# Weight parts of a fused attention and MLP kernel: one slot and one store for a high and low part, casts on ScalarE, later loads and sums

## The chip, the cores and the metric

The kernel runs on one core of one Trainium2 chip. The engines of the core are named as in the profile: PE (TensorE matmul), PEld (its weight loads), DVE (VectorE), ACT (ScalarE), POOL (GpSimd) and SP (SyncE, which issues all DMAs here, one after another). Each engine works through its own instructions strictly in the order in which the program lists them. The metric is the device time in microseconds of one execution; the median of three runs of the kernel before is 1123.24 us (1121.22 to 1124.15).

## The reference

Causal attention with a decay over 8 batches, 8 heads, 576 positions and 64 dimensions, followed by a two-layer MLP over the 4608 tokens:

```python
scores = scale * np.matmul(q, k.transpose(0, 1, 3, 2))
cum = np.cumsum(np.log(np.clip(f, 0.0001, 1.0)), axis=-1)
scores = np.where(causal, -1000000000.0, scores + cum[:, :, :, None] - cum[:, :, None, :])
attn = softmax(scores)                                  # max, exp, sum + 1e-9
x = np.matmul(attn, v) reshaped to (4608, 512)
h = x @ w_in                                            # (4608, 2048)
g = h * erf(np.maximum(h, 0.0) + np.log1p(np.exp(-np.abs(h))))
out = g @ w_out                                         # (4608, 512), float32
```

The weights w_in and w_out are given as float64 and read as pairs of 32-bit words.

## The kernel before, in words

**Attention.** The 64 heads go in 32 pairs, each pair in two steps `t` (even: query blocks 4 and 1, odd: 3, 2 and 0), so there are 64 steps and a tail of 5. It is a pipeline: in step t PE makes the scores of t (`scores`, line 607), DVE reduces them with the decay mask (`reduce`, 630), ACT takes the exponentials of t-1 (`exps`, 644), POOL normalizes t-2 (`normalize`, 651), PE transposes t-3 into one of three PSUM banks (`transposes`, 661), ACT and DVE copy these out (`evacuate`, 672), and PE multiplies t-4 with the values (`values`, 683). The last copy of `evacuate` on ACT must be done before PE's next use of that bank. POOL also makes the mask of step t+1 (`mask`, 592) from the cumulative decays c, which for all pairs but the first are read back from `cum_d`, the sums of all heads that the start of the program writes to memory.

**Early weight work.** One after another, small pieces of work on the weights are put behind the steps: `todo` (lines 516 and 792) has 60 of them, one popped in each step and two in each tenth step. Ten pieces of weights (eight of w_in, two of w_out for half 0) are loaded (`load`), then `magnitude` (ACT), `normal`, `low_bits` and `join` (DVE) turn the 64-bit words into float32, and `parts` (412) splits the result into a high part in float32r and a low part, the rest: the high by a cast, the low by a subtraction on POOL that reads the high part. For w_in four sums of quarters (`sums`) are split too, since the first product is computed by seven smaller products. The buffers of this work are slots xs1, xs2 (raw words), xs3, xs4 (top words) and xs6 (sums); the same slots hold later x's parts 1, 2, 3, 4 and 6. x's first group is read and split in `x_work`, from step 24 in even steps, and `start_x` (545), in steps 59 to 63: its j-th call casts part 1, 4, 6, 2 or 3 on ACT and takes the rest on POOL.

**The MLP.** It runs in units n of `step` (277), four for each of 12 visits v (six groups of tokens, twice, for the two halves of the hidden width; k is n modulo 4). A unit has seven products i = 0 to 6 (`product`), each of six matmuls, with two PSUM banks in turn. Their results are taken out by `consume`: a copy `sa` on ACT at i = 0 (line 194), an addition `sb` on DVE at i = 1, h copied on ACT at i = 2 (199), `sc` and three h on DVE at i = 3 to 6 (205). PE cannot start a product in a bank before the one that was there has been taken out. For the unit before, ACT takes softplus (209) and erf (212), each with its table load, DVE multiplies (215), ACT casts the high part gh (224) and POOL makes the low part gl (225). For the unit before that, PE makes the second product into y (242), six matmuls after each of i = 0, 1, 2, 3, 4 and 6.

What else is done stands in the order written here. `next_x` (128) reads and splits the x of the next visit: two sums by `x_sum` (lines 107 and 109) of the four blocks t0 to t3 that `load_x` has loaded, then casts on ACT and rests on DVE in the last unit of the visit. `late_work` (489) plans the weights of half 1 and the rest of half 0: piece m has a unit n, three places (a, b, c) for `normal`, `low_bits` and `join`, and a unit and place for its parts. In four rounds of four units each, piece pairs of w_in give seven parts (three quarters and four sums), whose casts (420) and subtractions (421) follow each other behind the products i = 3 to 6; they are stored to `wi_d` and read back by `reload` when half 1 begins. Their buffers lhi and llo share four rotating slots, `ws`; a slot is free when the store that reads it is done.

## Time and profile before

| | |
|---|---|
| median of 3 runs | 1123.24 us |
| the profiled execution | 1124.44 us |
| its span, first to last instruction | 1122.7 us |
| busy, share of the span | PE 97%, PEld 84%, DVE 70%, ACT 70%, POOL 47% |
| mean granted clock of TensorE | 0.992 |
| attention | to about 317 us, mixed with the first units to 353 us |
| full units without weight work (700 to 1000 us) | PE busy 300 of 300 us |

Times in the timelines are microseconds from the start of the span. A timeline row gives start, length, engine, line, instruction, the tiles, and in brackets how long the engine sat idle before it and what ended that. A row of waits gives the engine and line that waited, what it waited for, then total us, times and the longest. A row of the groups by form ends with total us and the mean in ns. The rows of the chip's DMAs end with KB each and the median us from issue to landing. A window row gives start and end, length, then the busy us of each engine with the count of instructions, the granted clock of TensorE, and the DMA share and GB/s.

### The profile page before, as it was taken

The page shows a single profiled execution, that of the slowest core. Times are in us where ns is not written, and L with a number is a line of the kernel's source. Part 1 is how long each engine was busy: PE and PEld are TensorE (multiplying, and loading weights), DVE is VectorE, ACT ScalarE, POOL GpSimd, SP SyncE. Part 2 cuts the span into 40 slices and gives each one's busy share as a digit, 9 for nine tenths or more (in the row PEclk, how much of TensorE's full clock was granted, in tenths as well). Part 3 has the DMA queues.
Part 4 walks back from the last instruction along what each step waited for, and adds up shares of the span by engine and source line. Part 5 has one row for each costly group of instructions (what it writes and reads, how often), then busy time and mean ns, then how long its engine had stood idle before and what let it go on. Part 6 is the DMA issues. An engine that isn't in the chain of part 4 may idle for free.

```text
span 1122.7 us, 21302 instructions
## 1 busy us (share of the span) xinstructions
PE 1084.4 (97%) x7384; PEld 945.6 (84%) x7384; DVE 781.1 (70%) x1776; ACT 782.1 (70%) x1718; POOL 533.2 (47%) x733
## 2 busy tenths in 40 slices
PE   8999999999998899998999989999999999999997
PEld 7888888888888788887878879889888988899886
DVE  5898999999855775785757765655656565656543
ACT  4888887878876676767667586666666576756662
POOL 4787979888853343343342533333223332233322
PEclk9999999999998999999999999999999999999999
DMA  7777886677433134152432417442221313040122
GB/s 252 237 244 234 274 271 245 223 246 221 136 111 104 39 130 141 41 176 96 164 118 82 154 48 262 175 176 81 85 85 57 113 57 114 15 138 18 31 82 75
DMA packets 74906, 155.82 MB, mean 139 GB/s; under 512 B 7472, under 2 KB 27184, under 8 KB 73776
## 3 DMA queue, kind: packets, MB, share of 16 engines
q1 hardware_dynamic: 74800, 154.47, 41.2%
q8 instruction: 59, 0.97, 0.3%
q14 instruction: 47, 0.39, 0.1%
HBM read 114.44 MB, written 39.99 MB: 138 GB/s over the span
## 4 chain that ended last, share of the span: by engine, by line
PE 67%; issue 17%; POOL 8%; DMA 3%; DVE 3%; ACT 1%; SPq 0%; POOLq 0%; DVEq 0%; ACTq 0%
PE y L242 22%; PE m L181 20%; PE s L616 8%; PE o L697 8%; PE t L670 7%; POOL gl L225 5%; POOL llo L421 2%; DMA wi_d<-llo 1%; DVE pr L636 1%; DMA xt_d<-xo 1%; PE s L620 1%; POOL wo L421 1%; PE idle L735 0%; DMA lraw<-in_w_out_dram 0%; ACT e L212 0%
## 5 line engine op out<-in xcount | busy, mean ns | idle before, releaser
L225 POOL TENSOR_TENSOR gl<-e,gh 128x384 fp32r<-128x384 f32 x192 | 224.4, 1197 | 489.8 <-ACT gh L224 476.2
L181 PE MATMUL m<-x,wi 128*128 128x384 f32 x2016 | 402.5, 338 | 19.0 <-ACT sa L194 9.2
L181 PEld LDWEIGHTS m<-x,wi 128*128 128x128 f32 x2016 | 358.2, 189 | 52.3 <-DVE h L205 15.0
L242 PE MATMUL y<-wo,gh 128*128 128x512 f32 x1152 | 359.2, 393 | 1.9 <-POOL wo L421 1.2
L242 PEld LDWEIGHTS y<-wo,gh 128*128 128x128 f32 x1152 | 212.7, 188 | 30.5 <-POOL wo L421 1.6
L242 PE MATMUL y<-wo,gl 128*128 128x512 f32 x576 | 228.9, 397 | 0.0
L658 POOL TENSOR_SCALAR pr<-pr,st 128x576 f32<-128x576 f32 (+4 forms) x320 | 165.1, 540 | 46.4 <-DVE st L654 22.3
L648 ACT ACTIVATE pr<-pr,st 128x576 f32<-128x576 f32 (+3 forms) x320 | 176.7, 557 | 5.7 <-DVE st L636 5.7
L215 DVE TENSOR_TENSOR e<-e,h 128x384 f32<-128x384 f32 x192 | 144.4, 793 | 28.2 <-ACT e L212 28.2
L636 DVE CUSTOM_DVE_ANT_0 pr<-s,c 128x576 f32<-128x576 f32 (+3 forms) x320 | 136.4, 486 | 21.8 <-PE s L620 13.8
L209 ACT ACTIVATE e<-h 128x384 f32<-128x384 f32 x192 | 93.4, 520 | 69.6 <-DVE h L205 69.2
L224 ACT CAST gh<-e 128x384 fp32r<-128x384 f32 x192 | 92.0, 512 | 59.6 <-DVE e L215 59.0
L242 PEld LDWEIGHTS y<-wo,gl 128*128 128x128 f32 x576 | 108.2, 188 | 23.0
L616 PE MATMUL s<-k,q 64*128 64x320 f32 (+4 forms) x768 | 110.0, 407 | 3.0 <-DVE st L636 3.0
L679 ACT COPY pt<-t 128x512 f32<-128x512 f32 x128 | 74.1, 579 | 54.5 <-PE t L670 52.4
L197 DVE TENSOR_TENSOR sb<-m,sa 128x384 f32<-128x384 f32 x48 | 26.7, 556 | 122.1 <-PE m L181 76.0
L697 PE MATMUL o<-pt,v 128*64 128x128 f32 (+1 forms) x1920 | 104.1, 261 | 3.7 <-DVE xo L706 2.4
L670 PE MATMUL t<-ident,pr 128*128 128x128 f32 x800 | 104.5, 276 | 3.0 <-ACT pt L679 2.9
L697 PEld LDWEIGHTS o<-pt,v 128*64 128x64 f32 x1920 | 95.2, 139 | 13.8 <-DVE st L636 4.2
L670 PEld LDWEIGHTS t<-ident,pr 128*128 128x128 f32 x800 | 87.4, 140 | 15.2 <-issue 10.7
L616 PEld LDWEIGHTS s<-k,q 64*128 64x128 f32 x768 | 72.6, 186 | 31.4 <-issue 16.7
L122 DVE TENSOR_TENSOR x<-t,x 128x768 fp32r<-128x768 f32 x77 | 80.3, 1054 | 18.9 <-ACT x L117 18.9
(96 smaller groups left out, 1098.3 us busy)
## 6 DMA issues: line engine op xcount, KB each, us to landing
v<-in_vp_dram SPq DMA_DIRECT2D x32, 576.0 KB, 6.9
c<-cum_d SPq DMA_DIRECT2D x62, 288.0 KB, 5.7
t<-xt_d SPq DMA_DIRECT2D x44, 384.0 KB, 5.8
q<-in_q_dram SPq DMA_DIRECT2D x32, 320.0 KB, 3.9
k<-in_k_dram SPq DMA_DIRECT2D x32, 288.0 KB, 4.5
xt_d<-xo SPq DMA_DIRECT2D x32, 288.0 KB, 6.0
part_d<-yo SPq DMA_DIRECT2D x36, 256.0 KB, 4.2
yo<-part_d SPq DMA_DIRECT2D x36, 256.0 KB, 3.1
```

The lines of the kernel that those rows point to most:

```text
L181: nc.tensor.matmul(out=ps, lhsT=w[:, wp, ws], rhs=x[:, xp, kd], start=first and kd == 0 and j == 0, stop=kd == 1 and j == 2 and i in (1, 2 ...
L209: self.nc.scalar.activation(out=e, in_=self.h[n, q], func=AF.Softplus)
L215: self.nc.vector.tensor_mul(self.e[n, q], self.e[n, q], self.h.pop((n, q)))
L224: nc.scalar.copy(out=gh, in_=e)
L225: nc.gpsimd.tensor_tensor(out=gl, in0=e, in1=gh.bitcast(F32), op=ALU.subtract)
L242: yield nc.tensor.matmul(out=y[tb], lhsT=g[:, cs], rhs=w[:, f, wp], start=first, stop=last)
L616: nc.tensor.matmul(out=s[j][:, at:at + k1 - k0], lhsT=q[h, PAD + START[i]:PAD + END[i]], rhs=k[h, k0:k1], start=i > 0, stop=i not in (0, 3))
L636: nc.vector.tensor_tensor_reduce(out=to[:, ::-1] if j else to, in0=score, in1=decay_, scale=-0.125, scalar=BIG, op0=ALU.add, op1=ALU.min, ...
L648: nc.scalar.activation(out=seg, in_=seg, func=AF.Exp, bias=st[:, 0, j, m:m + 1], scale=-1.0, accum_out=st[:, 1, j, m:m + 1])
L658: nc.gpsimd.tensor_scalar(out=seg, in0=seg, scalar1=st[:, 2, j, m:m + 1], scalar2=1.0, op0=ALU.mult, op1=ALU.mult)
L670: nc.tensor.transpose(out=b[:, n * P:(n + 1) * P], in_=probs[t][:, at:at + P], identity=ident)
L697: nc.tensor.matmul(out=o[h, to:to + width], lhsT=v[:, ch, h], rhs=pt[:, at[j]:at[j] + width], start=n == 0, stop=n == len(parts) - 1, skip ...
```

## The change

Five things change; PE's instructions and their order stay as they are.

- **One slot, one store.** For parts of w_in that go to memory, the high and low part are the two halves of one tile `both` (2 KB per partition) in one slot of `ws`, and one DMA of 256 KB stores them, where there were two tiles, two slots and two DMAs of 128 KB.
- **Early casts on ACT.** The high parts of the early weight work are cast by ACT (`nc.scalar.copy`) and not by DVE. At the start, the factor -8 of the decays is applied by ACT too.
- **The start.** q and k of pairs 1 and 2 and the first values are loaded ahead of everything that needs the decays; `load_decay` loads c apart. All three logarithms come first, then all three scans. The early weight work starts at step 6 instead of 3, and its first two loads are issued in steps 3 and 5. So it ends in step 60, where it ended in step 57.
- **x's sums of the second group.** `load_x` loads the blocks of the second 384 tokens (t2, t3) first. For visit 1 the two sums move from behind the products 4 and 5 of unit 2 to behind product 6 of unit 2 and product 0 of unit 3.
- **Weight pieces four and five of the late plan** (counted from 0): `normal`, `low_bits` and `join` of piece 4 move from products 5, 5 and 6 of unit 3 to 0, 0 and 1 of unit 4; those of piece 5 from 2, 2 and 4 of unit 4 to 4, 4 and 5.

```diff
@@ load_x, next_x
-        for j, (token, half) in enumerate([(0, 0), (0, 1), (1, 0), (1, 1)]):
+        for j in (2, 3, 0, 1):
+            token, half = divmod(j, 2)
...
-        if k == 2 and i in ((4, 5) if v == 1 else (0, 1)):
-            self.x_sum(v, i - (4 if v == 1 else 0), dve)
+        for j in range(2):
+            if (k, i) == ([(2, 6), (3, 0)][j] if v == 1 else (2, j)):
+                self.x_sum(v, j, dve)
@@ parts, in_parts
-            width = 512 if cut is None else 2 * P
             if to is not None:
                 hi, lo = to
+            elif cut:
+                both = buf("both", m, [P, 2, 2 * P], F32R)
+                hi, lo = both[:, 0], both[:, 1]
             else:
-                hi, lo = (buf(x, m, [P, width], F32R) for x in ("hi", "lo"))
+                hi, lo = (buf(x, m, [P, 512], F32R) for x in ("hi", "lo"))
...
-            if to is None:
+            if to is None and cut:
+                nc.sync.dma_start(out=dst, in_=both.bitcast(F32))
+            elif to is None:
                 nc.sync.dma_start(out=dst[0], in_=hi.bitcast(F32))
                 nc.sync.dma_start(out=dst[1], in_=lo.bitcast(F32))
@@ late_buf
-        tag, bufs = {"raw": ("raw", 2), "top": ("top", 3), "tt": ("tt", 1), "hi": ("ws", 4), "lo": ("ws", 4)}[kind]
+        tag, bufs = {"raw": ("raw", 2), "top": ("top", 3), "tt": ("tt", 1), "hi": ("ws", 4), "lo": ("ws", 4),
+                     "both": ("ws", 4)}[kind]
@@ early_work, late_work
-            pieces, early_buf, nc.vector.tensor_copy)
+            pieces, early_buf, nc.scalar.copy)
...
-        plan = [(1, first, 2, 1), (1, second, 2, 1), (2, first, 3, 2), (2, second, 3, 3), (3, (5, 5, 6), 4, 2), (4, first, 4, 5)]
+        plan = [(1, first, 2, 1), (1, second, 2, 1), (2, first, 3, 2), (2, second, 3, 3), (4, (0, 0, 1), 4, 2), (4, (4, 4, 5), 4, 5)]
...
-            moe.work[n, "abs"].append(lambda m=m: magnitude(m))
+            moe.work[n - (m == 4), "abs"].append(lambda m=m: magnitude(m))
@@ decay, load, load_decay
-            nc.vector.tensor_scalar(out=out, in0=out, scalar1=-8.0, scalar2=None, op0=ALU.mult)
+            nc.scalar.activation(out=out, in_=out, func=AF.Copy, scale=-8.0)
...
-            c = io.tile([P, 2, S], F32, name=f"c{p}", tag="c")
-            if p:
-                for j in range(2):
-                    n = 2 * p + j
-                    nc.sync.dma_start(out=c[:, j], in_=cum_d[n:n + 1].rearrange("a s -> (a s)").partition_broadcast(P))
-            pairs[p] = [q, k, c]
+            pairs[p] = [q, k, io.tile([P, 2, S], F32, name=f"c{p}", tag="c")]
+
+        def load_decay(p):
+            c = pairs[p][2]
+            for j in range(2):
+                n = 2 * p + j
+                nc.sync.dma_start(out=c[:, j], in_=cum_d[n:n + 1].rearrange("a s -> (a s)").partition_broadcast(P))
@@ the start and the steps
+        for p in (1, 2):
+            load(p)
+        load_values(0)
         idle_products("", 34)
-        log_clipped(fd[0])
-        log_clipped(fr)
+        for x in (fd[0], fr, fd[1]):
+            log_clipped(x)
         decay(pairs[0][2][:, 0], fd[0])
         cum = wk.tile([B * H, S], F32, name="cum", tag="xo")
         decay(cum, fr)
         nc.sync.dma_start(out=cum_d, in_=cum)
-        load(1)
-        load(2)
-        load_weight(0)
-        load_weight(1)
+        for p in (1, 2):
+            load_decay(p)
         mask(0, slice(0, 1))
-        log_clipped(fd[1])
+        decay(pairs[0][2][:, 1], fd[1])
+        mask(0, slice(1, 2))
...
-                if t >= 3 and todo:
+                if t >= 6 and todo:
                     todo.pop(0)()
+            if t in (3, 5):
+                load_weight(t // 2 - 1)
```

Where the order of the instructions moves, three places matter for what follows. Tile names carry the step or unit, then a running number.

The end of attention, on ACT, at the end of step 60 (x0_4 is x's part 4, whose slot is xs4; top9 are the top words of the last weight piece, in the same slot; wo0_0 its high and low part; pr60 the scores of step 60; pt58 the transposed ones of 58). Before:

```order
L679 COPY pt57_5088<-t57_1_5094 128x512
L117 CAST x0_4_5138<-tc_2177 128x768
L648 ACTIVATE pr60_5081,st60_5082<-pr60_5081,st60_5082 128x576
L648 ACTIVATE pr60_5081,st60_5082<-pr60_5081,st60_5082 128x192
L679 COPY pt58_5168<-t58_0_5169 128x512
```

Now:

```order
L688 COPY pt57_5085<-t57_1_5091 128x512
L424 CAST wo0_0_4564<-top9_4891 128x512
L118 CAST x0_4_5138<-tc_2168 128x768
L657 ACTIVATE pr60_5078,st60_5079<-pr60_5078,st60_5079 128x576
L657 ACTIVATE pr60_5078,st60_5079<-pr60_5078,st60_5079 128x192
L688 COPY pt58_5168<-t58_0_5169 128x512
```

The cast of the last weight piece has come in front of x's part 4; that cast now waits on POOL for the subtraction that still reads top9.

The end of unit 2 and the start of unit 3, on DVE (ltop2 and ltop3 are late weight pieces, h2_1 and h2_2 the results of the products 5 and 6, t1_4 and t1_2 the two sums of x). Before:

```order
L107 TENSOR_TENSOR t1_4_5729<-t1_2_5727,t1_3_5728 128x768
L409 SCALAR_TENSOR_TENSOR ltop2_5793<-ltop2_5793,lraw2_5717 128x512
L397 SCALAR_TENSOR_TENSOR ltop3_5795<-ltop3_5795,lraw3_5719 128x512
L205 TENSOR_TENSOR h2_1_5866<-m2_2_5815,sb2_5770 128x384
L109 TENSOR_TENSOR t1_2_5727<-t1_0_5725,t1_2_5727 128x768
L402 TENSOR_SCALAR lraw3_5719<-ltop3_5795 128x512
L404 SCALAR_TENSOR_TENSOR lraw3_5719<-lraw3_5719 128x512
L205 TENSOR_TENSOR h2_2_5877<-m2_3_5840,sb2_5770 128x384
L409 SCALAR_TENSOR_TENSOR ltop3_5795<-ltop3_5795,lraw3_5719 128x512
```

Now:

```order
L411 SCALAR_TENSOR_TENSOR ltop2_5793<-ltop2_5793,lraw2_5717 128x512
L399 SCALAR_TENSOR_TENSOR ltop3_5795<-ltop3_5795,lraw3_5719 128x512
L207 TENSOR_TENSOR h2_1_5865<-m2_2_5815,sb2_5770 128x384
L404 TENSOR_SCALAR lraw3_5719<-ltop3_5795 128x512
L406 SCALAR_TENSOR_TENSOR lraw3_5719<-lraw3_5719 128x512
L207 TENSOR_TENSOR h2_2_5875<-m2_3_5840,sb2_5770 128x384
L108 TENSOR_TENSOR t1_4_5729<-t1_2_5727,t1_3_5728 128x768
L411 SCALAR_TENSOR_TENSOR ltop3_5795<-ltop3_5795,lraw3_5719 128x512
L110 TENSOR_TENSOR t1_2_5727<-t1_0_5725,t1_2_5727 128x768
```

Both sums, which need x from memory, now stand behind both h, which free PE's banks.

The start, on DVE (fd0 and fd1 are the decays of the first two heads, fr those of all heads, c0 and cum their sums). Before:

```order
L563 TENSOR_SCALAR fd0_155<-fd0_155 128x576
L563 TENSOR_SCALAR fr_158<-fr_158 64x576
L568 SCALAR_TENSOR_TENSOR c0_164<-fd0_155 128x576
L569 TENSOR_SCALAR c0_164<-c0_164 128x576
L568 SCALAR_TENSOR_TENSOR cum_207<-fr_158 64x576
L569 TENSOR_SCALAR cum_207<-cum_207 64x576
L563 TENSOR_SCALAR fd1_156<-fd1_156 128x576
```

Now:

```order
L570 TENSOR_SCALAR fd0_155<-fd0_155 128x576
L570 TENSOR_SCALAR fr_158<-fr_158 64x576
L570 TENSOR_SCALAR fd1_156<-fd1_156 128x576
L575 SCALAR_TENSOR_TENSOR c0_164<-fd0_155 128x576
L575 SCALAR_TENSOR_TENSOR cum_221<-fr_158 64x576
L575 SCALAR_TENSOR_TENSOR c0_164<-fd1_156 128x576
```

The clip of fd1 stands ahead of the scans, and the multiplications by -8 are no longer on DVE.

## The prediction

> **What bounds the kernel now.** I read the busy times by stretch first, then the waits of TensorE, then the timelines around its gaps. In attention, from 40 to 280 us:

> ```profile
> 40.00:280.00 240.00, 239.52 (x2784) 199.03 (x2782) 226.28 (x838) 197.37 (x615) 205.58 (x386) 1.00 0.76 246
> ```

> The columns after the length are PE, PEld, DVE, ACT, POOL, then clock and DMA. PE is busy 239.5 of 240 us, so shortening another engine's work buys almost nothing there; DVE is at 94%, ACT at 82%, so DVE is next. What can be won is where PE waits. Its waits over the whole run, longest first, with one of ACT beside them:

> ```profile
> PE m L181 <- ACT sa L194: 9.2, 4, 2.7
> PE m L181 <- DVE h L205: 9.1, 10, 1.5
> ACT pt L679 <- PE t L670: 52.4, 57, 2.5
> ```

> The first row is four gaps of about 2.3 us, the second ten shorter ones. The third says that in attention ACT waits for PE about 0.9 us in nearly every step: ACT has a little slack and not more.

> **The weight rounds (one slot per part).** In each of four rounds, ACT makes seven high parts and POOL seven low ones. Before, each took one of four slots, so two parts were in flight. Round one:

> ```profile
> 432.54 0.71 ACT L420 CAST lhi<-ltop 128x256 fp32r<-128x256 f32 x2
> 435.32 2.07 POOL L421 TENSOR_TENSOR llo<-ltop,lhi 128x256 fp32r<-128x256 f32 x2
> 442.25 0.41 ACT L420 CAST lhi<-ltt 128x256 fp32r<-128x256 f32 x1 [0.79 <-DMA wi_d<-lhi]
> 442.56 0.93 ACT L209 ACTIVATE e<-h 128x384 f32<-128x384 f32 x2
> 443.40 0.46 ACT L194 COPY sa<-m 128x384 f32<-128x384 f32 x1
> 443.91 1.33 PE L181 MATMUL m<-x,wi 128*128 128x384 f32 x6 [2.01 <-ACT sa L194]
> ```

> The seventh cast starts at 442.25, 9.7 us after the first, because each waits for stores; two softplus and the copy sa stand behind it on ACT, and PE, ready at 441.90, waits for sa. Now four casts run at once (done by 434.2), and the fifth needs the store of part one, which needs the low part, which needs POOL. POOL still begins at 435.32; its low parts end at 436.25, 437.4 and, at about 0.9 each, 438.3. The store is one of 256 KB:

> ```profile
> wi_d<-lhi SPq DMA_DIRECT2D x28, 128.0 KB, 1.7
> wo_d<-lhi SPq DMA_DIRECT2D x8, 256.0 KB, 2.3
> part_d<-yo SPq DMA_DIRECT2D x36, 256.0 KB, 4.2
> ```

> The wo_d row has the same size and shape, so 2.3: slots come free at 438.6, 439.7 and 440.6; the seventh cast ends at 441.0, softplus 0.93 later, sa at 442.4. PE then waits 0.5 instead of 2.0. For four rounds: 9.2 - 4 x 0.5 = **7.2 us gained**. Bounds: with 4.2 us (the part_d row) the last slot comes at 442.5 and the gain is 0; with no wait left it is 9.2. The 28 stores fewer cost SP nothing that PE waits for.

> **The first units (x sums, weight pieces five and six).** The chain in units 2, 3 and 4:

> ```profile
> 366.58 1.01 DVE L107 TENSOR_TENSOR t<-t,t 128x768 f32<-128x768 f32 x1 [3.04 <-DMA t<-xt_d]
> 368.72 0.55 DVE L205 TENSOR_TENSOR h<-m,sb 128x384 f32<-128x384 f32 x1
> 369.32 1.33 PE L181 MATMUL m<-x,wi 128*128 128x384 f32 x6 [1.51 <-DVE h L205]
> 387.13 1.75 DVE L397 SCALAR_TENSOR_TENSOR ltop<-ltop,lraw 128x512 f32<-128x512 f32 x1
> 388.38 0.50 PE L242 MATMUL y<-wo,gh 128*128 128x512 f32 x1 [1.17 <-POOL wo L421]
> 389.99 0.55 DVE L205 TENSOR_TENSOR h<-m,sb 128x384 f32<-128x384 f32 x1
> 390.59 1.50 PE L181 MATMUL m<-x,wi 128*128 128x384 f32 x6 [1.48 <-DVE h L205]
> ```

> DVE sits 3.04 us at the sum of x for its load, and h, which frees PE's bank, stands behind it. With the sums behind both h (and tokens' second half loaded first) h is done near 366 and 367.6, PE's 1.51 go, and the sums find their data. Softplus of that h then comes earlier too: erf, gates and POOL's wo parts of unit 3 move about 2 us against 1.5 for PE, so of the 1.17 some 0.5 go. In unit 3 the piece's normal (387.13, 1.75 us) and low bits stood ahead of h at 389.99; they now follow in unit 4, so the 1.48 go. After these gaps PE ran slowly:

> ```profile
> 392.00:394.00 2.00, 2.00 (x6) 1.54 (x5) 1.83 (x4) 1.99 (x4) 0.00 (x0) 0.50 0.44 135
> 394.00:396.00 2.00, 2.00 (x10) 1.84 (x9) 2.00 (x4) 1.43 (x4) 0.00 (x0) 0.76 0.33 127
> 646.00:650.00 4.00, 1.50 (x8) 1.46 (x9) 0.56 (x1) 3.14 (x7) 1.45 (x2) 1.00 0.48 168
> ```

> Granted clock 0.50 and 0.76 for 2 us each: 1.0 + 0.5 = 1.5 us lost, which should not recur without the gaps (the third row, a gap of 2.7 in a round, kept 1.00, so a gap does not always cost it). [...] The trace has 0.50 right behind them, so I keep the row's term. Against it: DVE has no idle time in unit 4, and the moved work puts wo's second piece for unit 5 later there; I take off 0.2. Together 1.5 + 0.5 + 1.5 + 1.5 - 0.2 = **4.8 us gained**; bounds 1.5 (only the first gap) and 5.7.

> **Attention: cast by ACT.** 30 casts leave DVE:

> ```profile
> L420 DVE CAST wi<-tt 128x256 fp32r<-128x256 f32 x16 | 6.9, 470 | 0.0
> ```

> At most 0.47 each, 14 us off an engine that runs beside a full PE. ACT gets about as much; where a cast follows join in the same step, ACT also waits for DVE's join, with the next exponentials behind it. ACT's 0.9 us a step covers most of that. The work starts three steps later, and one step now carries all four sums on DVE. I take +0.3, between -2 and +2. But the last piece now ends in step 60, where it ended in 57, and there it meets x's split. Step 60, and two durations:

> ```profile
> 300.85 0.83 ACT L117 CAST x<-tc 128x768 fp32r<-128x768 f32 x1
> 303.04 0.21 DVE L675 COPY pt<-t 128x64 f32<-128x64 f32 x1
> 303.54 1.82 POOL L122 TENSOR_TENSOR x<-tc,x 128x768 fp32r<-128x768 f32 x1
> 305.05 0.59 ACT L679 COPY pt<-t 128x512 f32<-128x512 f32 x1 [2.15 <-PE t L670]
> 305.33 2.86 POOL L658 TENSOR_SCALAR pr<-pr,st 128x448 f32<-128x448 f32 x6
> 309.60 0.59 ACT L679 COPY pt<-t 128x512 f32<-128x512 f32 x1
> 310.56 1.54 PE L697 MATMUL o<-pt,v 128*64 128x128 f32 x28
> L409 DVE SCALAR_TENSOR_TENSOR top<-top,raw 128x512 int32<-128x512 int32 x10 | 8.9, 890 | 0.0
> L420 ACT CAST lhi<-ltop 128x512 fp32r<-128x512 f32 x8 | 4.9, 616 | 0.0
> L421 POOL TENSOR_TENSOR wo<-top,wo 128x512 fp32r<-128x512 f32 x2 | 2.6, 1280 | 1.4 <-DVE st L653 1.4
> ```

> Slot xs4 holds this piece's top words and then x's part 4. So ACT's cast of x, today at 300.85, waits for POOL's wo, which waits for ACT's cast of wo, which waits for DVE's join, behind the copy at 303.04: 303.25 + 0.89 + 0.62 + 1.28 = 306.1, and the cast of x ends near 307.0. Behind it on ACT stand the exponentials and evacuations of the next step (5.4 us later); on POOL x's rest and then the normalization, 305.33 now, near 308.9 then. It ends at 311.8. The copy at 309.60, which frees the bank for the last transpose ahead of PE's values, ends 8.5 us after the cast of x now, 2.15 of them waiting; with 6.35 of work it ends at 313.4 and values start at 313.5 instead of 310.56: 3.0 us lost. Such a gap costs up to 1.8 us of clock or none (rows above): 0.9. **3.9 us lost**, between 0 (the slack takes it) and 6.

> **The start.** The first clips, and what waits for the decays:

> ```profile
> 2.88 0.43 SPq L722 DMA_DIRECT2D fd<-in_f_dram  x1
> DMA to landing us min/median/max: 4.9/4.9/4.9
> L568 DVE TENSOR_TENSOR_SCAN c<-fd 128x576 f32<-128x576 f32 x2 | 2.7, 1344 | 0.0
> L564 ACT ACTIVATE fd<-fd 128x576 f32<-128x576 f32 x2 | 1.4, 684 | 6.8 <-DVE fd L563 6.8
> 13.52 0.76 DVE L636 CUSTOM_DVE_ANT_0 pr<-s,c 128x576 f32<-128x576 f32 x1 [0.40 <-POOL c L603]
> 18.53 0.88 POOL L603 TENSOR_SCALAR_AFFINE_SELECT c<-c 128x256 f32<-128x256 f32 x2 [3.80 <-DMA c<-cum_d]
> ```

> The third clip now stands ahead of all scans and waits for its load, 2.88 + 4.9 = 7.8; with 0.5 and three scans of 1.34 DVE is at 12.3, ACT scales by 13.0 (0.68), POOL masks, and the second head's reduction starts near 13.6, as today. The store of the sums slips from 9.9 to about 11.7, behind five loads that now go ahead; its readers may land 2 us later than 18.53, where step 2 needs its mask by about 21.5. I take **0.2 lost**, between 2 lost and 0.5 gained.

> **Sum.** 7.2 + 4.8 + 0.3 - 3.9 - 0.2 = 8.2 us. The span of 1122.7 becomes 1114.5; the profiled run was 1124.44, 1.7 more than its span, and 1.2 above the median of 1123.24. On the median: **1115.0 us**.

> **Rivals.**
> - The wait at step 60 is absorbed and the rounds lose their whole gap: 8.2 + 3.9 + 2.0 = 14.1, 1109.1. For it: pipelines of five steps. Against: ACT's slack is 0.9 us a step and the delay 5.4. Chance 0.13.
> - The stores take the gain: a slot is now held through POOL and a longer store; at 4.2 us the 7.2 vanish: 1.0 is left, 1122.2. For it the part_d row, against it the wo_d row of equal shape. Chance 0.10.
> - The reordered work only moves waits: the first units keep their gaps (DVE is full from 381 to 404) and the loss at step 60 stays: 7.2 - 3.9 - 1.5 = 1.8, 1121.4. Chance 0.07.
> - Slower: ACT becomes attention's pace. It gets 30 casts (13 us at about 0.42) and six waits for join of about 1.1 us (its 0.89 and the copies ahead of it), and its 52.4 us of waiting are spread evenly, so lumps may pass to PE. If all of that reaches PE it is 20 us against 12 gained elsewhere: 1123.2 + 20 + 0.2 - 12 = 1131; it decides once over 12 us pass. Against: PE 239.5 of 240 busy beside an ACT at 82%. Chance 0.08.
> - The clock's drop at 392 has another cause than the gaps and stays: 1.5 less, 1116.5. For it the row of 646, where a longer gap kept 1.00. Chance 0.12. [...]

> The forecast itself has 0.50. About 0.3% (3.4 us) can be told from no change, so faster means below 1119.9: the forecast, the clock rival and the first, 0.75; the second and third lie within, 0.17; slower 0.08. Range 1108 to 1122: it holds the first rival's edge and the second's; the forecast's own is 1111 to 1120.

> **What would show it.** Right: in the four rounds PE's wait for sa near 0.5; no wait for h at units 3 and 4 and a clock of 1.00 between 380 and 400; a wait of PE or ACT for POOL's wo or its bank near the end of attention, about 3 us. Wrong: stores of 256 KB landing near 4 us, PE below 99% busy between 40 and 280, or step 2 waiting for its decays.

## The result

The changed kernel takes 1112.71 us in the median (1111.97 to 1114.95, four runs) against 1122.23 (1120.22 to 1124.15) of the kernel before in the same session: a ratio of 0.9919, 95% interval 0.9895 to 0.9943. Six more runs of the same kernel in a later session gave 0.9939 (0.9927 to 0.9951). One execution of the kernel oddx below, at 1321.85 us and a mean clock of 0.751, was in a slow state and stands outside its ratio. The forecast was 1115.0 in a range of 1108 to 1122, so it held, 2.3 us too high. The executed span of the profiled run fell from 1122.7 to 1111.0.

PE's waits over the whole run, after the change (the engine and line that waits, what it waits for, total us, times, longest; lines have moved by two to nine):

```profile
PE m L183 <- DVE h L207: 7.0, 9, 1.3
PE t L679 <- ACT pt L688: 4.5, 4, 2.7
PE s L625 <- DVE st L645: 3.3, 3, 2.7
PE m L183 <- ACT sa L196: 1.5, 4, 0.4
PE y L244 <- POOL wo L425: 1.0, 2, 0.6
ACT pt L688 <- PE t L679: 35.5, 45, 2.6
```

The wait for sa, 9.2 before, is 1.5 now, 0.4 in each of the four rounds; the forecast had 0.5. The wait for h fell from 9.1 to 7.0; 5.3 of the 7.0 are one wait of 1.3 us in each round, 10 us behind the wait for sa, which the kernel before has too. New is more waiting for ACT's copy pt (4.5, before 2.9). ACT still waits 35.5 us for PE's transposes (52.4 before), so it is not attention's pace. Round one in the timelines of ACT and PE:

```profile
428.98 1.02 ACT L424 CAST lboth<-ltop 128x256 fp32r<-128x256 f32 x3
429.90 0.40 ACT L424 CAST lboth<-ltt 128x256 fp32r<-128x256 f32 x1
434.81 0.41 ACT L424 CAST lboth<-ltt 128x256 fp32r<-128x256 f32 x1 [4.51 <-DMA wi_d<-lboth]
437.06 0.41 ACT L424 CAST lboth<-ltt 128x256 fp32r<-128x256 f32 x1 [0.73 <-DMA wi_d<-lboth]
438.72 1.32 PE L183 MATMUL m<-x,wi 128*128 128x384 f32 x6 [0.39 <-ACT sa L196]
```

and its stores among the DMA issues (KB each, median us from issue to landing):

```profile
wi_d<-lboth SPq DMA_DIRECT2D x28, 256.0 KB, 2.0
```

Four casts run at once, the fifth waits 4.51 us for the first store (POOL only begins its low parts at 431.76), and the seventh comes 8.1 us after the first, where it came 9.7 after. The 256 KB land in 2.0 us.

At step 60 the slot made the chain that was foreseen; in the timelines of ACT and POOL:

```profile
301.76 0.62 ACT L424 CAST wo<-top 128x512 fp32r<-128x512 f32 x1 [2.93 <-DVE top L411]
303.76 0.83 ACT L118 CAST x<-tc 128x768 fp32r<-128x768 f32 x1 [1.39 <-POOL wo L425]
306.46 2.85 POOL L667 TENSOR_SCALAR pr<-pr,st 128x448 f32<-128x448 f32 x6
```

ACT's cast of wo waits 2.93 us for DVE's join, and behind it the cast of x 1.39 us for POOL's wo.

To see where time came from, I follow six moments of PE's timeline through all kernels: the start of the scores of step 4 and of step 62, the first product into y, the end of the wait for sa in rounds one and four, and the span. The labels after the first two rows are those of the experiments below (after_2 is the changed kernel again).

| kernel | step 4 | step 62 | first y | round 1 | round 4 | span |
|---|---|---|---|---|---|---|
| before | 27.15 | 307.35 | 352.98 | 443.91 | 648.50 | 1122.7 |
| after | 26.47 | 305.22 | 353.32 | 438.72 | 637.17 | 1111.0 |
| after_2 | 29.17 | 307.82 | 353.68 | 439.07 | 637.52 | 1111.5 |
| u_rounds | 29.58 | 308.13 | 353.96 | 440.96 | 645.83 | 1120.0 |
| u_units | 29.43 | 308.16 | 353.98 | 444.18 | 642.67 | 1116.7 |
| u_plan | 28.66 | 307.74 | 354.19 | 441.00 | 639.49 | 1113.5 |
| u_start | 26.23 | 304.83 | 350.67 | 436.06 | 634.60 | 1108.6 |
| bridge | 26.18 | 305.24 | 352.75 | 439.09 | 637.58 | 1111.5 |
| u_cast | 29.24 | 308.56 | 354.20 | 439.63 | 638.12 | 1111.9 |
| oddx | 28.42 | 307.68 | 356.23 | 441.67 | 640.19 | 1114.2 |
| fix60 | 29.35 | 311.24 | 354.43 | 439.87 | 638.31 | 1112.3 |
| topslot | 28.72 | 307.40 | 354.24 | 439.66 | 638.12 | 1112.1 |
| best | 25.47 | 307.47 | 351.30 | 436.64 | 635.15 | 1109.0 |
| best_bridge | 24.94 | 305.62 | 349.59 | 435.01 | 633.50 | 1107.4 |

In the first profile the change brought 0.7 us up to step 4, 1.45 from there to step 62 and 5.5 between y and round one, 6.1 between rounds one and four; it lost 2.5 between step 62 and y. The sum, 11.3, is nearly the whole 11.7 of the spans. The medians differ by 9.5 only, since the profiled execution of before was itself 2.2 slower than its median.

### The profile page after: what moved, and what is told of

The parts are those of the page before. It is cut to its first block, busy times and chain, and to the rows that moved or that the text cites. A ratio compares the mean times of both kernels' runs of the same rounds, so it can differ in the third digit from the quotient of the medians.

```text
span 1111.0 us, 21223 instructions
## 1 busy us (share of the span) xinstructions
PE 1080.9 (97%) x7384; PEld 942.5 (85%) x7384; DVE 768.7 (69%) x1743; ACT 791.9 (71%) x1751; POOL 534.0 (48%) x733
## 4 chain that ended last, share of the span: by engine, by line
PE 72%; ACT 8%; issue 7%; DVE 6%; POOL 4%; DMA 2%; POOLq 0%; SPq 0%; DVEq 0%; ACTq 0%
PE y L244 25%; PE m L183 23%; PE s L625 8%; PE o L706 8%; PE t L679 7%; POOL gl L227 2%; ACT e L214 1%; DVE e L217 1%; POOL lboth L425 1%; ACT L214 1%; ACT e L211 1%; ACT pr L657 1%; DVE pr L645 1%; ACT x L118 1%; DMA wi_d<-lboth 1%
## 5 line engine op out<-in xcount | busy, mean ns | idle before, releaser
L679 PE MATMUL t<-ident,pr 128*128 128x128 f32 x800 | 105.1, 276 | 5.4 <-ACT pt L688 4.5
L679 PEld LDWEIGHTS t<-ident,pr 128*128 128x128 f32 x800 | 87.4, 140 | 18.3 <-issue 9.9
L688 ACT COPY pt<-t 128x512 f32<-128x512 f32 x128 | 73.8, 577 | 38.3 <-PE t L679 35.5
## 6 DMA issues: line engine op xcount, KB each, us to landing
part_d<-yo SPq DMA_DIRECT2D x36, 256.0 KB, 4.1
yo<-part_d SPq DMA_DIRECT2D x36, 256.0 KB, 3.0
```

Source lines behind the costliest of these rows:

```text
L679: nc.tensor.transpose(out=b[:, n * P:(n + 1) * P], in_=probs[t][:, at:at + P], identity=ident)
```

## The experiments

Twelve kernels, each timed in turn with the kernel before; ratios are against that. The kernel after_2 is the changed kernel unedited; best and best_bridge carry two and three edits, and each of the others changes or takes back one part. A way "from y to round one" is the time between two columns of the table.

**The rounds alone taken back (u_rounds).**

```diff
-            elif cut:
-                both = buf("both", m, [P, 2, 2 * P], F32R)
-                hi, lo = both[:, 0], both[:, 1]
             else:
-                hi, lo = (buf(x, m, [P, 512], F32R) for x in ("hi", "lo"))
+                hi, lo = (buf(x, m, [P, 2 * P if cut else 512], F32R) for x in ("hi", "lo"))
...
-            if to is None and cut:
-                nc.sync.dma_start(out=dst, in_=both.bitcast(F32))
-            elif to is None:
-                nc.sync.dma_start(out=dst[0], in_=hi.bitcast(F32))
-                nc.sync.dma_start(out=dst[1], in_=lo.bitcast(F32))
+            if to is None:
+                for j, x in enumerate((hi, lo)):
+                    nc.sync.dma_start(out=dst[:, j] if cut else dst[j], in_=x.bitcast(F32))
```

> The changed kernel with its one slot and one store taken back: high and low part of w_in's late weights again have a slot each of the four and a store each of 128 KB; all else stays. Theory A (the four rounds gained by the slots): the four waits of PE for sa return, about 2.3 us each, round spacing goes from 66.15 back to about 68.2, and the time is 1112.7 + 7 = about 1119.7 (1118 to 1121). Theory B (most of the gain of the rounds came from the earlier units, whose stores and loads reach them earlier): the waits stay below 1 us each, and the time is within 3 us of 1112.7.

Measured: 1121.39, ratio 1.0001 (0.9989 to 1.0014): without this part the rest of the change is, in sum, worth nothing. PE's waits for sa and for h in this kernel:

```profile
PE m L183 <- ACT sa L196: 9.5, 4, 3.0
PE m L183 <- DVE h L207: 1.9, 6, 0.8
```

and the window over the rounds (length, then PE, PEld, DVE, ACT and POOL busy, granted clock, DMA share, GB/s):

```profile
440.00:700.00 260.00, 250.13 (x1193) 219.08 (x1194) 180.06 (x260) 186.86 (x336) 103.32 (x91) 0.97 0.37 127
```

From y to round one it takes 87.00 against 85.39 in after_2, from round one to four 204.87 against 198.45: 1.6 + 6.4 = 8.0 us. This is theory A, though the time lies just above its 1118 to 1121; by the ratios the part is worth 7.0 us against after_2 and 9.2 against the first timing. The clock in this stretch was 0.97 here and 1.00 in the kernel before, yet the rounds lie as far apart in both (204.87 and 204.59): behind the wait for sa PE ran slower (the six matmuls took 1.32 to 1.56 us, 1.31 to 1.33 in the kernel before), and then the wait of 1.3 us for h, 10 us later in each round of the kernel before, was gone.

**The first units taken back, and one half of them (u_units, u_plan).** u_units puts back load_x, next_x and the plan; u_plan the plan only:

```diff
-        plan = [..., (4, (0, 0, 1), 4, 2), (4, (4, 4, 5), 4, 5)]
+        plan = [..., (3, (5, 5, 6), 4, 2), (4, first, 4, 5)]
...
-            moe.work[n - (m == 4), "abs"].append(lambda m=m: magnitude(m))
+            moe.work[n, "abs"].append(lambda m=m: magnitude(m))
```

> The changed kernel with the first units taken back: the order of x's four loads, the places of the two sums of visit 1, and the places of weight pieces four and five are as before; all else stays. Theory A (gaps and the clock behind them are one mechanism): the waits of PE for h at units 3 and 4 return (1.5 us each), wo's at unit 3 grows by 0.5, the new waits at unit 5 (0.83 and 0.39) go, and the granted clock falls again to about 0.5 and 0.76 behind them: 1112.7 + 1.5 + 0.5 + 1.5 + 1.5 - 1.2 = 1116.5. Theory B (the clock's fall is not tied to these gaps): 1115.0 with a clock of 1.00 between 390 and 396.

> The changed kernel with only weight pieces four and five of the late plan put back (piece 4's normal, low bits and join in unit 3, piece 5's behind the products 2 and 4 of unit 4); x's loads and sums stay as changed. Theory A (the gaps of units 3 and 4 add up, and the clock falls behind the pair of gaps of 1.2 and 1.5 us at 388 to 391): the way from the first product into y to the first round takes 85.4 + 1.5 (gap) + 0.5 (wait for wo) + 1.5 (clock) - 1.2 (unit 5) = 87.7, against 90.2 with x's sums put back too, so the sums' part is 2.5; the clock falls below 0.9 between 380 and 400. Theory B (the clock falls only where the gap at 369 came before): the clock stays at 1.00 there and the way takes 86.2.

Measured: u_units 1118.39, ratio 0.9964 (0.9950 to 0.9978); u_plan 1114.19, 0.9931 (0.9917 to 0.9946), which alone can't be told from the changed kernel. The time of u_units is above both theories. In the trace the way from y to round one takes 90.20 in u_units, 86.81 in u_plan and 85.39 in after_2: 4.8 for both, 1.4 for the plan, 3.4 for the sums. Up to 1.7 of the 3.4 is not the sums' own: in the profile of u_units the clock was at half for 6.8 us, in u_plan's for 3.4. The twelve executions of u_units fall in two groups, four from 1113.9 to 1114.9 and eight from 1117.2 to 1119.7, and the profiled one is of the second; so the part is worth less than 4.8 in a third of the executions. That the clock makes the two groups is likely, but only one of them was profiled. The gaps in u_units' timeline, and the windows behind them:

```profile
389.10 0.50 PE L243 MATMUL y<-wo,gh 128*128 128x512 f32 x1 [1.16 <-POOL wo L424]
391.31 2.29 PE L182 MATMUL m<-x,wi 128*128 128x384 f32 x6 [1.48 <-DVE h L206]
```

```profile
392.00:394.00 2.00, 2.00 (x7) 1.90 (x7) 1.90 (x4) 1.97 (x3) 0.00 (x0) 0.50 0.08 26
394.00:396.00 2.00, 2.00 (x7) 1.52 (x6) 1.68 (x4) 2.00 (x5) 0.00 (x0) 0.50 0.67 249
```

The same two views of u_plan:

```profile
387.28 0.50 PE L244 MATMUL y<-wo,gh 128*128 128x512 f32 x1 [0.62 <-POOL wo L425]
389.49 2.29 PE L183 MATMUL m<-x,wi 128*128 128x384 f32 x6 [1.47 <-DVE h L207]
```

```profile
390.00:392.00 2.00, 2.00 (x8) 1.90 (x7) 1.90 (x4) 1.97 (x4) 0.00 (x0) 0.50 0.07 14
392.00:394.00 2.00, 2.00 (x10) 1.72 (x9) 1.67 (x4) 2.00 (x5) 0.00 (x0) 0.87 0.75 259
```

And of after_2, where the waits of unit 5 come later:

```profile
390.00:392.00 2.00, 2.00 (x12) 1.78 (x11) 2.00 (x5) 2.00 (x4) 0.00 (x0) 1.00 0.02 4
392.00:394.00 2.00, 2.00 (x12) 1.82 (x11) 2.00 (x4) 1.97 (x4) 0.03 (x1) 1.00 0.00 0
```

```profile
401.51 1.33 PE L183 MATMUL m<-x,wi 128*128 128x384 f32 x6 [0.80 <-DVE h L207]
404.13 0.50 PE L244 MATMUL y<-wo,gh 128*128 128x512 f32 x1 [0.36 <-POOL wo L425]
```

In the three profiles that have the pair of gaps (before, u_units, u_plan) the clock fell to 0.50 between 388 and 398, in the eleven without it stood at 1.00 from 380 to 400. This is theory A as far as the clock goes; u_plan's 86.8 lies between the two theories' 87.7 and 86.2. The sizes differ: the clock fell for 6.8 us in u_units and 3.4 in u_plan, and the new waits at unit 5, 0.80 + 0.36, are six times what the forecast took off (0.2).

**The changed kernel again (after_2), and the start taken back (u_start).** u_start has the old order of loads, logarithms and sums at the start; the factor on ACT and the later weight work stay:

```diff
-        for p in (1, 2):
-            load(p)
-        load_values(0)
         idle_products("", 34)
-        for x in (fd[0], fr, fd[1]):
-            log_clipped(x)
+        log_clipped(fd[0])
+        log_clipped(fr)
...
         for p in (1, 2):
+            load(p)
             load_decay(p)
         mask(0, slice(0, 1))
-        decay(pairs[0][2][:, 1], fd[1])
-        mask(0, slice(1, 2))
+        log_clipped(fd[1])
...
-            if half == 0 and there[2] and p > 1:
+            if half == 0 and there[2]:
...
                 reduce(t, 0)
+                if t == 0:
+                    decay(pairs[0][2][:, 1], fd[1])
+                    mask(0, slice(1, 2))
```

> The changed kernel itself once more, unedited, so that single parts taken back can be set against it over more executions. Theory A (the clock's fall behind the first wait of 3 us in the start comes in some executions and not in others, and the first profile was one without): some executions show a start as in the runs with parts taken back, step 2 at about 22.4 and not 19.16, and the times spread over about 3 us, with a median of 1112 to 1114. Theory B (the fall belongs to the edited kernels): step 2 starts near 19.2 again and the times stay within 1 us.

> The changed kernel with the start taken back: loads of pairs 1 and 2 and of the first values behind the store of the decays again, the second head's logarithm and sums behind the first reductions; the factor -8 stays on ACT, the early weight work stays at step 6. Theory A (the start's 0.8 us came from the clock, which stayed at 1.00 behind a gap of 2.7 us, and the order itself cost about 0.5): 1112.7 - 0.5 if the clock stays at 1.00 between 16 and 20, up to 1113.5 if it falls again to 0.52 and 0.62. Theory B (the earlier loads themselves gain time in the first steps): step 3 starts later than in the changed kernel by more than what the clock costs, and the time is 1114 or more.

Measured: u_start 1110.07, ratio 0.9900 (0.9885 to 0.9915), so it is faster than the changed kernel as timed again (0.9939; 0.9927 to 0.9951). PE's timeline at the start of after_2, a window of it, and the timeline of u_start:

```profile
14.13 4.44 PE L625 MATMUL s<-k,q 64*128 64x448 f32 x12 [3.54 <-DVE st L645]
18.68 3.53 PE L744 MATMUL idle<-ident 128*128 128x128 f32 x18
22.14 1.57 PE L625 MATMUL s<-k,q 64*128 64x320 f32 x12
```

```profile
16.00:18.00 2.00, 2.00 (x8) 1.51 (x5) 0.00 (x0) 0.26 (x2) 0.00 (x0) 0.50 0.98 280
```

```profile
13.79 1.73 PE L625 MATMUL s<-k,q 64*128 64x448 f32 x10 [2.01 <-DVE st L645]
15.64 3.64 PE L744 MATMUL idle<-ident 128*128 128x128 f32 x18
19.21 1.56 PE L625 MATMUL s<-k,q 64*128 64x320 f32 x12
```

The new order lets PE wait 3.54 us in one piece, the clock is at 0.50 for 6.8 us, and scores of 1.7 and idle transposes of 2.1 us take 4.4 and 3.5. Step 4 comes 2.9 us later than with the old order. The six times of after_2 lie between 1112.89 and 1114.32: so of theory A for it one part stands (the fall exists in the unedited kernel) and one does not (the spread is 1.4, not 3). Neither theory for u_start had its size. Where the clock stays at 1.00, step 4 starts at 26.47 (after) or 26.18 (bridge) with the new order and at 25.47 (best) or 24.94 (best_bridge) with the old, so the order itself costs about 1 us. The fall costs 2.7 us more with the new order (29.17) and about 1 with the old (26.23).

**Filling the wait (bridge).**

```diff
-                    idle_products(t, 18)
+                    idle_products(t, 44 if t == 0 else 18)
```

> The changed kernel with 44 instead of 18 idle transposes behind the scores of step 0, 26 more of about 0.12 us, which fill the wait of about 3 us in which PE waits for the second head's first reduction. Theory A (the idle stretch drops the clock): the clock stays at 1.00 from 12 to 24, the scores of step 2 start at 19.2 at the latest, and against the changed kernel in executions with the fall it gains 3 us, with a smaller spread between executions. Theory B (the clock falls for another reason, the load of DMAs or transposes that do not count as work): the clock is again near 0.50 from 15 to 22 and step 2 starts at 22.4 or later.

Measured: 1113.47, ratio 0.9946 (0.9930 to 0.9962): no gain. But its start did what theory A said; PE's timeline at the start and in round one, then windows at the end of attention:

```profile
15.06 1.69 PE L625 MATMUL s<-k,q 64*128 64x448 f32 x10 [0.23 <-DVE st L645]
18.88 2.04 PE L625 MATMUL s<-k,q 64*128 64x320 f32 x12
439.09 1.31 PE L183 MATMUL m<-x,wi 128*128 128x384 f32 x6 [1.32 <-ACT sa L196]
```

```profile
335.00:340.00 5.00, 2.53 (x9) 2.12 (x11) 1.03 (x2) 2.44 (x7) 0.00 (x0) 0.69 0.01 3
340.00:345.00 5.00, 5.00 (x39) 4.88 (x38) 2.38 (x5) 3.70 (x6) 1.55 (x2) 0.63 0.00 0
```

Step 2 starts at 18.88 and not at 22.14, and step 62 2.6 us earlier than in after_2. In this profile the lead was then given back: the clock fell behind the 2.7 us wait near 337 (it stayed at 1.00 there in after_2), and the last 0.9 went in round one, where the seventh cast waited 1.67 us for its store and not 0.75, so that PE waited 1.32 for sa. Why the median of six executions did not gain is not shown by one profile and stays open.

**Attention: casts back on DVE (u_cast), x's loads and splits in odd steps (oddx).**

```diff
-            pieces, early_buf, nc.scalar.copy)
+            pieces, early_buf, nc.vector.tensor_copy)
```

```diff
-            if t >= 24 and t % 2 == 0 and x_work:
+            if t >= 24 and t % 2 == 1 and x_work:
```

> The changed kernel with the casts of the early weight work on DVE again; the steps of the work and all else stay. Theory A (the casts' engine matters little, what shortened attention from step 4 to step 62 by 1.5 us was that the work moved by three steps against the odd and even steps): that stretch stays within 0.7 of 278.7 and the time within 1 us of the changed kernel, a little less where the chain join, cast, subtraction at the end is shorter by ACT's turn. Theory B (DVE's relief is the gain): the stretch returns to about 280.2 and the time rises by 1.5 or more.

> The changed kernel with the loading and splitting of x's first group popped in the odd steps from 25 and not in the even ones from 24; all weight work stays in its step. Theory A (attention's 1.5 us from step 4 to step 62 came from the shift by three steps, which parted ACT's magnitudes, now in steps 41, 45, 53 and 57, from ACT's casts of x in even steps): now the casts of x fall on steps 41, 43, 53 and 55, two of them with a magnitude, as before the change; the stretch rises from 278.65 to about 280 and the excess over 9.46 per pair of steps stands at 40 to 44 and 52 to 56. Theory B (the shift gained because pieces no longer met at other places, or by DVE's relief): the stretch stays within 0.5 of 278.65.

Measured: u_cast 1114.33, ratio 0.9951 (0.9936 to 0.9965); oddx 0.9940 (0.9925 to 0.9955). From step 4 to 62 u_cast takes 279.32, oddx 279.26, after_2 278.65, before 280.20. So of the 1.55 us that attention gained, 0.67 go with the casts and some 0.6 with the way in which weight work and x's splits fall on the steps: in oddx one pair of steps (40 to 42) takes 10.00 in place of 9.46, where a magnitude and a cast of x meet on ACT. The stretch of u_cast fits its theory A and the time its theory B; the stretch of oddx lies between its two. Since oddx moves x's work and not the weight work, it tests the shift only indirectly. The two effects may overlap, and neither can be told from nothing in the median.

**The end of attention: three extra double steps (fix60), another slot (topslot).**

```diff
-            for _ in range(1 + (t % 10 == 0)):
+            for _ in range(1 + (t % 10 == 0 or t in (15, 25, 35))):
```

```diff
-        slot = {"raw": (1, 2)[m % 2], "top": (3, 4)[m % 2], "tt": 6}[kind]
+        slot = {"raw": (1, 2)[m % 2], "top": 6 if m == 9 else (3, 4)[m % 2], "tt": 6}[kind]
```

> The changed kernel with three more steps that carry two pieces of the early weight work (steps 15, 25 and 35), so that its last piece ends in step 57, as before the change, and not in step 60; ACT still casts. Theory A (the loss at the end of attention is the meeting of the last piece with x's split in one slot): ACT's casts of x no longer wait for POOL's wo, the scores of the steps 62 and 63 start 4.7 us apart and not 7.3, and the time is 1112.7 - 2.6 = about 1110.1. Theory B (ACT's cast of wo itself, in whichever step, holds up the exponentials): a stall of about the same size moves to the step of the last piece, and the time stays within 1 us of 1112.7.

> The changed kernel with one number changed: the top words of the last early piece lie in slot xs6 (free since the sums of step 50; x's part 6 needs it in step 61) and not in xs4, which x's part 4 needs in step 60; the steps of all work stay. Theory A (the meeting in the slot is the loss): from the start of the scores of step 62 to the first product into y it takes 43.2 as where the work ended in step 57, and not 45.8, and the time falls by 2.6. Theory B (ACT's casts and POOL's subtraction of wo hold up the pipeline themselves): the stretch stays near 45.8 and the time stays.

Measured: fix60 1113.92, ratio 0.9934 (0.9920 to 0.9947); topslot 1113.55, 0.9939 (0.9926 to 0.9952); neither differs from the changed kernel. In fix60 the way from step 62 to y takes 43.19 against 45.86 in after_2, both at a clock of 1.00: the meeting costs 2.7 us. But from step 4 to 62 fix60 takes 281.89, 3.2 longer. The largest part of it, 1.3, is lost in the steps 42 to 44 (10.88 in place of 9.58), where a cast on ACT waits for DVE's join ahead of a copy that PE needs (timelines of ACT and PE). That the rest comes from weight work meeting x's split in other steps is argued, not shown.

```profile
213.80 0.41 ACT L424 CAST wi<-top 128x256 fp32r<-128x256 f32 x1 [1.88 <-DVE top L411]
216.36 0.30 PE L679 MATMUL t<-ident,pr 128*128 128x128 f32 x1 [0.89 <-ACT pt L688]
```

In topslot the wait for POOL's wo is gone, and the wait for the join stays (timelines of ACT and PE, then windows); in u_cast, where DVE makes the cast of wo, it is the other way round (the last timeline, of ACT):

```profile
303.95 0.62 ACT L424 CAST wo<-top 128x512 fp32r<-128x512 f32 x1 [2.99 <-DVE top L411]
304.48 0.84 ACT L118 CAST x<-tc 128x768 fp32r<-128x768 f32 x1
311.55 0.30 PE L679 MATMUL t<-ident,pr 128*128 128x128 f32 x1 [0.75 <-ACT pt L688]
```

```profile
320.00:340.00 20.00, 17.31 (x149) 16.09 (x147) 7.65 (x20) 11.82 (x26) 7.92 (x14) 0.95 0.27 102
340.00:360.00 20.00, 17.13 (x120) 15.31 (x119) 12.41 (x22) 12.17 (x22) 5.96 (x6) 0.88 0.17 56
```

```profile
306.94 0.83 ACT L118 CAST x<-tc 128x768 fp32r<-128x768 f32 x1 [4.79 <-POOL wo L425]
```

PE's waits between 307 and 314 fell from 1.9 us in after_2 to 0.9, and the scores of the steps 62 and 63 start 5.85 us apart where it was 7.33 in after_2 and 4.68 in fix60; so taking the slot away gains a little over half of the loss. Taking ACT's cast away and leaving the slot, as u_cast does, gains almost nothing: 7.16 between the two steps, and 45.64 from step 62 to y. The two parts do not add up: while the slot is shared, the chain through it makes the wait by itself. In the profile of topslot the gain does not reach y, since the clock fell to 0.95 and 0.88 there: up to 20 x 0.05 + 20 x 0.12 = 3.4 us.

**Towards a faster kernel (best, best_bridge).** The old start with double steps only at 54 and 57, so that the steps up to 53 keep their order; best_bridge adds idle transposes:

```diff
-            for _ in range(1 + (t % 10 == 0)):
+            for _ in range(1 + (t % 10 == 0 or t in (54, 57))):
...
-                    idle_products(t, 18)
+                    idle_products(t, 35 if t == 0 else 18)
```

> The changed kernel with the old start (as in the run with the start taken back) and two more steps with two pieces of the early weight work, 54 and 57, so that the last piece ends in step 58, before x's split of part 1; the steps up to 53 stay as changed. Theory A (loss at the end is the meeting of the last piece with start_x; the steps up to 53 keep their gain): from step 62 to the first y 43.2 to 44, the stretch from step 4 to 62 within 0.7 of 278.6, time 1110.1 - 2 = about 1108. Theory B (each added double step costs attention what the end gains, as with doubles at 15, 25 and 35): 1110, no change against the run with the old start.

> As the run before it, with 35 instead of 18 idle transposes behind the scores of step 0, which fill the 2.0 us in which PE waits for DVE there. Theory A (that stretch of idleness halves the clock for some 4 us): the clock stays at 1.00 from 12 to 22, step 2 starts at 17.4 and not at 19.2, and the time falls by 1.8, unless the clock then falls at another gap (near 340 or 350), where it costs as much again. Theory B: no change at step 2.

Measured: best 1111.46, ratio 0.9907 (0.9888 to 0.9925), no better than u_start: theory B in its outcome, though the end went as theory A said (43.83 from step 62 to y). From step 4 to y it takes 325.83 against 324.44 in u_start; steps 56 to 58 take 10.4 in place of 9.5, PE waits 2.0 us for DVE's copy xo at 299, and the clock was 0.91 between 300 and 320, 0.96 behind. best_bridge 1110.76, 0.9897 (0.9880 to 0.9913): step 2 starts at 17.63 and the span is the shortest of all, 1107.4. u_start and best_bridge cannot be told from each other; both beat the changed kernel as timed again by about 0.4%, though not beyond the interval of its first timing (0.9895 to 0.9943).

## Why the prediction was right, and where it was not

The total came right by the two large terms, and by errors of the small ones that partly cancelled.

- **Rounds, forecast 7.2.** Measured 8.0 by taking the part back, in one profile (7.0 and 9.2 by the two ratios). The row of wo_d was the right one to price the store: 2.0 us where 2.3 was taken, and a rest of 0.4 per round where 0.5 was. The rival that stores take the gain, and its 4.2 us, falls.
- **First units, forecast 4.8.** Measured 4.8 in one profile. The gaps and the clock behind them were the mechanism, but two sizes were off against each other, and that they cancel is luck. The clock's part was larger (0.50 for 6.8 us in u_units, up to 3.4 us of loss, where 1.5 was taken from the profile of before), and the waits that reappear in unit 5 were 1.2, not 0.2. The rival that reordered work only moves waits holds for these 1.2.
- **The clock rival falls.** At units 3 and 4 the clock fell in the three profiles with the pair of gaps and in none of the eleven without. It does not fall behind every gap: in the rounds of the kernel before it stayed at 1.00 behind waits of 2.0 to 2.7 us. In u_plan it fell to 0.50 with 0.62 and 1.47 us of waiting and 0.7 us of work between them.
- **Casts, forecast 0.3 gained.** Attention gained 1.55 between step 4 and 62. The step that failed is the one that counted the shift by three steps as nothing: about 0.6 us came from where pieces meet x's work, 0.7 from the casts, as far as two profiles tell. (The 14 us taken off DVE are nearer 11: from 40 to 280 us it was busy 215.2 us and not 226.3.) ACT as attention's pace, the slower rival, falls: PE stayed at 239.4 of 240 us busy.
- **End of attention, forecast 3.9 lost.** The chain was as foreseen, its cost 2.7: the 3.0 of waiting was nearly right, the 0.9 of clock didn't come (1.00 from 300 to 320 in both profiles of the changed kernel). This 0.9 was half of 1.8, which the rows named for it do not give: they add up to 1.5. The rival that the wait is absorbed falls. The chain through the slot makes the wait also with the cast on DVE (u_cast); without the slot 1.2 of the 2.7 us between the steps 62 and 63 are left, where ACT's cast of wo still waits for DVE's join. That this wait is their cause is argued, since no run takes both away and leaves the work in step 60.
- **Start, forecast 0.2 lost.** This is the term that failed: 2.0 lost up to step 4 against before (after_2), 2.9 against the old order in the same kernel. The forecast had the second head's reduction "near 13.6, as today", and it came at about 14.1; but it did not look at PE, which now waits once for 3.5 us where it waited 0.4 and 2.2, and it charged no clock, though the same text did so for gaps half as long at 390. The first profile, with a wait of 2.74, happened to keep the clock and would have hidden this; the last section has an estimate of why.

With these sizes the sum is 8.0 + 4.8 + 1.5 - 2.7 - 2.0 = 9.6 where 8.2 was forecast; the ratios of the two sessions are worth 9.1 and 6.8 us of 1122. The terms come from single profiles, and what makes the second session's gain smaller than their sum is not shown.

## What to carry to other kernels

Before a buffer is enlarged, look at what its slots wait for: here pairing two halves in one slot doubled what could be in flight, and nearly the whole gain of the change hung on it. When an instruction that waits for another engine moves to a new engine, count what stands behind it there (at step 60 ACT's cast of wo waited 2.93 us for DVE, with x's part 4 and the exponentials behind it), and look at which steps it now shares with other work; a shift by three steps moved as much as the change of engine. Where PE's waits are of the sizes behind which the clock fell to 0.50 here (2.01 us at once in u_start, 0.62 and 1.47 us close together in u_plan), price the clock behind them too, and time several executions before reading a gain of 3 us out of one profile.

## What the runs showed of the hardware

**When the clock falls.** The wait of PE for DVE in the start, with the length of the gap and what the clock did behind it, over fourteen profiles: 0.2 (bridge and best_bridge) and 1.70 us (best): 1.00; 2.01 (u_start), 2.22 (before), 2.42 (oddx), 2.45 (topslot) and 2.61 (u_plan): a fall to 0.50; 2.74 (after): 1.00; 3.13 (fix60), 3.54 (after_2), 3.75 (u_rounds), 3.77 (u_cast) and 3.79 (u_units): a fall to 0.50. So the length of a gap does not decide alone. Near 337 a gap of 2.7 us, the same in every kernel, was followed by a fall in the first profile of the changed kernel, where it ended at 337.38, and by 1.00 in the second, where it ended at 340.06 (windows of after, then of after_2):

```profile
335.00:340.00 5.00, 2.62 (x13) 2.21 (x15) 1.03 (x2) 2.62 (x7) 0.00 (x0) 0.76 0.00 0
```

```profile
340.00:345.00 5.00, 4.94 (x47) 4.53 (x47) 2.30 (x5) 3.51 (x6) 0.00 (x0) 1.00 0.01 3
```

```profile
12.67:16.08 3.41, 1.37 (x9) 1.14 (x9) 1.50 (x5) 1.30 (x4) 1.54 (x4) 1.00 0.79 237
16.10:19.50 3.40, 3.40 (x19) 3.28 (x18) 2.63 (x14) 2.00 (x7) 0.88 (x2) 0.50 0.95 345
644.15:647.56 3.41, 1.65 (x8) 1.04 (x6) 0.00 (x0) 1.34 (x4) 1.56 (x3) 1.00 0.66 230
647.56:650.98 3.42, 2.48 (x12) 2.27 (x13) 0.56 (x1) 3.39 (x7) 0.73 (x1) 1.00 0.33 115
```

The first gap lies whole in one piece, which leaves PE 1.37 us busy, and the next piece runs at 0.50. The second, longer gap is cut by the edge at 647.56, which leaves 1.65 and 2.48, and no fall comes. For the start of after there is an estimate: carried back from its fall at 337.59 in steps of 3.41 (10.24 / 3), an edge at 13.33 cuts its gap of 2.74 us, which ended at 14.13. In after_2 the fall at the start began near 14.72, worked out from the clock of 0.68 between 14 and 16, 1.4 us off that edge; so the edges lie differently in these two executions of one kernel, and as far as they go that is the part of chance. For the other profiles this division is not shown, nor is why a fall followed 1.71 us in before and none 1.76, or 1.94 in after. In u_rounds the clock was 0.91 in the 20 us around each of the rounds two to four, with waits for sa of 2.41, 2.00 and 3.04; in the kernel before, with 2.46, 2.04 and 2.70, it was 1.00.

**The clock stayed at 1.00 through transposes.** In bridge, PE had nothing but transposes of the identity from 8.87 to 13.84, and the clock stayed at 1.00 from 10 to 26, where in after_2, with a wait of 3.54 us in the place of the added ones, it had fallen to 0.50.

**In u_rounds a lost clock was hardly lost time.** The clock was 0.91 from 500 to 520, from 570 to 590 and from 640 to 660, up to 20 x 0.09 = 1.8 us of work in a round, and from round one to four it took 204.87 us against 204.59 in the kernel before at 1.00. PE waited as long for sa (9.5 and 9.2 us), but its waits for h fell from 9.1 to 1.9. So the mean clock alone did not tell here how much time it cost.
